# Retention and wave-MLP on one core: the first batch's pairs interleaved, idle products at the start, casts on other engines

## The chip, the cores and the metric

One core of a Trainium2 chip. The metric is the time of one execution on the device in microseconds (us): the median of several runs. The engines are called by the names of the profile: PE (TensorE, matrix products), DVE (VectorE), ACT (ScalarE), POOL (GpSimd) and SP (SyncE, which issues the transfers).

## What is computed

The inputs are q, k and v of 4 batches, 8 heads, 768 positions and 64 columns, and four weight matrices. A retention layer is followed by a mixing layer:

```
gamma = 1 - 2 ** (-5 - h)                       # one decay per head
for t in range(768):
    state = gamma * state + outer(k[t], v[t])   # 64 x 64 per batch and head
    y[t]  = (1 / 8) * q[t] @ state
x = y, heads side by side                       # 4 x 768 x 512
theta = x @ w_theta
zr, zi = x * cos(theta), x * sin(theta)
u = x + w_tok_r @ zr + w_tok_i @ zi             # mixing over the 768 positions
out = u + max(u @ w_ch, 0)
```

## The kernel before, in words

The positions are cut into chunks of 128, six for each batch, 24 in all; n counts them (L56, L61). Inside a chunk the recurrence is written as products: scores k·q under a causal mask, scores times v, and q times the state that the chunks before have left. The decays are put into q and v as factors (`qsc`, `vsc`, and `qscp`, `vscp` for pairs), computed at the start with Exp on ACT. Products take bf16 operands and add up in PSUM.

**An order by hand.** The kernel asks for manual scheduling (L66): each engine works through its instructions in the order in which the program text issues them, and a pool of tiles with a fixed number of buffers makes an instruction wait until the tile that held the buffer before has been read. PSUM is divided by tags: "tr" (two buffers, all transposes), "acc" (two: values `yT_ps`, `th_ps`, and some y and o products), "at", "st" and "y" (one each).

**Loads.** All loads of the head are issued at once on SP, in the order of the string at L120 (p for a pair, c for a chunk, w for two row blocks of the token matrices, th and ch for the two others). The loads of a w must wait until one of the four buffers `wtok` has been cast by `w_cast`, and those behind them in SP's queue wait too.

**The first batch, in pairs.** The six chunks of batch 0 are taken as three pairs g = 0, 1, 2. A pair's 256 positions lie as 128 partitions times two neighbours, so that a load has longer rows. `pair_in(g)` (L512) does all of a pair:

- `pair_prep` (L212): cast of k (one POOL instruction of 1024 columns), scaling of q and of v (two POOL instructions of 512 columns each).
- `pair_T` (L224): eight PE transposes of k or q to PSUM, one DVE copy back (`kqT`, L231).
- `pair_A(g, two)` (L234): sixteen small score products, then the mask multiply on DVE (L247). There is one PSUM buffer for scores, so the second set waits for the first mask.
- `pair_Y(g)` (L252): for both halves sixteen value products (L262); then for each chunk a of the pair in turn the four products with the state (L274), the eight products that add to the state (L282), two casts of the state by ACT into `stbd` (`state_out`, L296, L299), and the cast of the values to `xT` by ACT (L292).

Then `att_X(n)` (L367) follows for each chunk: four transposes of xT (L373) with a DVE copy to `x_sb` (L379), four products with w_theta (L376), and two sines on ACT, cos and sin (L381, L382). `att_Z` (L385) multiplies them with x on DVE into `z` (L387).

**Token matrices.** `w_cast(t0)` (L445) casts two row blocks on POOL into three buffers `wrow`; `w_tok(t0)` (L451) transposes them with twelve PE instructions (L455), and a DVE copy (wtr, L461) and an ACT copy (wti, L459) put them in place.

**Mixing.** `moe_M(m, lo, hi)` (L394) adds two y products per chunk of positions (L405), each 512 columns wide, and at the end u = y + x on DVE (L410). `moe_U` (L413) transposes u, `moe_O` (L426) multiplies with w_ch (L433), and DVE forms the output (L436), which SP stores.

**The order of the head**, L524 to L552: pair 0, the cast of w_theta on DVE (L525), `att_X` of chunks 0 and 1, pair 1, and so on, with y products of m = 0 and 1 put between as soon as their z and w are there. In the pairs 1 and 2 the z of the chunk before stands on DVE between the copies of k and q.

**The slot loop**, from L573: slot s does the scores of chunk n = 6 + s, the values of the chunk before, x and the sines of the one before that, z of the one before that, and one mixing row m in two halves. POOL scales chunk n + 1 (`att_prep`, L184 to L189). In slots 1, 3 and 5 `w_tok(3)`, `w_tok(4)` and `w_tok(5)` stand at L615, behind the products and ahead of the slot's `att_X`. `moe_U` stands at L595, ahead of `att_Yinter` (L323).

## Time and profile before

| | us |
|---|---|
| median of 9 runs (199.04 to 200.37) | 200.0 |
| the profiled execution | 199.31 |
| its span, first to last instruction | 197.5 |
| PE busy in the span | 164.2 |
| DVE / ACT / POOL busy | 105.1 / 76.3 / 77.1 |
| first score product of pair 0, 1, 2 | 10.44, 25.84, 42.50 |
| first y product of the slot loop | 61.41 |

A span is the profile's time base, and the profiled execution's own time is 1.81 us longer than it. The landmarks come from the timeline, which lists an engine's instructions in order of time: start, length, line, tile written <- tiles read, sizes, and in brackets how long the engine had been idle and which engine's instruction ended that. The stages list, for each stretch, busy time and number of instructions of PE, PEld (loads of the stationary operand), DVE, ACT and POOL, then the granted clock, the transfers' busy share and GB/s. The waits list who waited for whom: total, times, longest.

### The profile page before, as it was taken

The page shows a single profiled execution, that of the slowest core. Times are in us where ns is not written, and L with a number is a line of the kernel's source. Part 1 is how long each engine was busy: PE and PEld are TensorE (multiplying, and loading weights), DVE is VectorE, ACT ScalarE, POOL GpSimd, SP SyncE. Part 2 cuts the span into 40 slices and gives each one's busy share as a digit, 9 for nine tenths or more (in the row PEclk, how much of TensorE's full clock was granted, in tenths as well). Part 3 has the DMA queues.
Part 4 walks back from the last instruction along what each step waited for, and adds up shares of the span by engine and source line. Part 5 has one row for each costly group of instructions (what it writes and reads, how often), then busy time and mean ns, then how long its engine had stood idle before and what let it go on. Part 6 is the DMA issues. An engine that isn't in the chain of part 4 may idle for free.

```text
span 197.5 us, 3773 instructions
## 1 busy us (share of the span) xinstructions
PE 164.2 (83%) x1484; PEld 96.4 (49%) x1508; DVE 105.1 (53%) x147; ACT 76.3 (39%) x142; POOL 77.1 (39%) x107
## 2 busy tenths in 40 slices
PE   0447628945897897997999999999999999999991
PEld 0335425534553564654565566555555444444460
DVE  1162470362246747676787668666565554542451
ACT  4005804622531587536464464425643453200010
POOL 6849680300189882999255526525000000000000
PEclk9999985695799999999999999999999999999997
DMA  5999995199499999989496895994457446233343
GB/s 154 328 307 336 319 309 139 22 264 300 108 209 229 283 191 226 271 227 227 94 227 127 177 202 144 192 213 106 110 131 81 106 106 108 81 108 112 101 136 108
DMA packets 85906, 35.64 MB, mean 180 GB/s; under 512 B 70912, under 2 KB 80384, under 8 KB 85888
## 3 DMA queue, kind: packets, MB, share of 16 engines
q1 hardware_dynamic: 85744, 35.27, 77.5%
q8 instruction: 12, 0.20, 0.4%
q10 hardware_dynamic: 144, 0.13, 0.2%
q14 instruction: 6, 0.05, 0.1%
HBM read 25.69 MB, written 6.29 MB: 162 GB/s over the span
## 4 chain that ended last, share of the span: by engine, by line
PE 74%; DVE 9%; ACT 7%; DMA 3%; issue 3%; POOL 1%; DVEq 0%; SPq 0%; ACTq 0%; POOLq 0%
PE y_ps L405 29%; PE o_ps L433 10%; PE th_ps L376 10%; DVE at L247 4%; PE yT_ps L340 3%; DMA pair<-in_q_dram 3%; PE at_ps L311 3%; PE x_ps L373 2%; PE st_ps L282 2%; PE kq_ps L198 2%; PE w_ps L455 2%; ACT stbd L299 2%; PE st_ps L348 2%; DVE z L387 2%; PE at_ps L243 2%
## 5 line engine op out<-in xcount | busy, mean ns | idle before, releaser
L405 PE MATMUL y_ps<-z,wti 128*128 128x512 bf16 x136 | 52.0, 383 | 0.9 <-issue 0.4
L405 PE MATMUL y_ps<-z,wtr 128*128 128x512 bf16 x126 | 48.0, 381 | 1.1 <-DVE z L387 0.6
L381 ACT ACTIVATE cs<-th_ps,halfpi 128x512 bf16<-128x512 f32 x24 | 16.5, 688 | 36.1 <-PE th_ps L376 33.7
L387 DVE TENSOR_TENSOR z<-cs,x_sb 128x1024 bf16<-128x1024 bf16 x24 | 19.4, 807 | 16.2 <-ACT cs L382 16.2
L376 PE MATMUL th_ps<-wth,xT 128*128 128x512 bf16 x89 | 26.4, 407 | 0.7 <-issue 0.4
L299 ACT CAST stbd<-st_ps 64x256 bf16<-64x256 f32 x40 | 14.7, 366 | 30.0 <-PE st_ps L282 29.5
L315 DVE TENSOR_TENSOR at<-at_ps,mask 128x1024 bf16<-128x1024 f32 x18 | 21.9, 1219 | 5.6 <-PE at_ps L311 5.6
L433 PE MATMUL o_ps<-wch,uT 128*128 128x512 bf16 x89 | 23.2, 379 | 0.4 <-ACT cs L382 0.3
L410 DVE TENSOR_TENSOR u<-y_ps,x_sb 128x512 bf16<-128x512 f32 x23 | 15.8, 690 | 12.0 <-PE y_ps L405 11.8
L189 POOL TENSOR_TENSOR vb<-vf,vsc 128x512 bf16<-128x512 f32 x18 | 19.2, 1068 | 6.1 <-PE yT_ps L340 5.0
L448 POOL CAST wrow<-wtok 128x768 bf16<-128x768 f32 x12 | 9.8, 826 | 28.8 <-issue 27.2
L405 PEld LDWEIGHTS <-wti 128*128 128x128 bf16 x138 | 13.6, 98 | 15.3 <-issue 2.4
L436 DVE SCALAR_TENSOR_TENSOR ot<-o_ps,u 128x512 f32<-128x512 f32 x23 | 15.8, 690 | 9.8 <-PE o_ps L433 9.7
L405 PEld LDWEIGHTS <-wtr 128*128 128x128 bf16 x138 | 13.6, 98 | 13.6 <-issue 0.3
L187 POOL TENSOR_TENSOR kqb<-qf,qsc 128x512 bf16<-128x512 f32 x18 | 19.7, 1095 | 0.0
L186 POOL CAST kqb<-kf 128x512 bf16<-128x512 f32 x18 | 11.5, 637 | 18.9 <-issue 14.1
L379 DVE COPY x_sb<-x_ps 128x512 bf16<-128x512 bf16 x19 | 7.9, 418 | 18.0 <-PE x_ps L373 18.0
L382 ACT ACTIVATE cs<-th_ps,zerob 128x512 bf16<-128x512 f32 x24 | 16.4, 681 | 0.0
L356 ACT CAST xT<-yT_ps 128x512 bf16<-128x512 f32 x18 | 10.6, 587 | 11.8 <-PE yT_ps L340 11.6
L201 DVE COPY kqT<-kq_ps 128x1024 bf16<-128x1024 bf16 x13 | 9.0, 691 | 9.3 <-PE kq_ps L198 9.3
L433 PEld LDWEIGHTS <-uT 128*128 128x128 bf16 x92 | 8.8, 98 | 10.3 <-issue 0.6
L376 PEld LDWEIGHTS <-xT 128*128 128x128 bf16 x96 | 9.4, 107 | 8.0 <-issue 2.1
(73 smaller groups left out, 196.1 us busy)
## 6 DMA issues: line engine op xcount, KB each, us to landing
out_dram<-ot SPq DMA_DIRECT2D x23, 256.0 KB, 2.2
kf<-in_k_dram SPq DMA_DIRECT2D x18, 256.0 KB, 4.8
qf<-in_q_dram SPq DMA_DIRECT2D x18, 256.0 KB, 5.1
vf<-in_v_dram SPq DMA_DIRECT2D x18, 256.0 KB, 4.9
wtok<-in_moe_w_tok_r_dram SPq DMA_DIRECT2D x6, 384.0 KB, 5.5
wtok<-in_moe_w_tok_i_dram SPq DMA_DIRECT2D x6, 384.0 KB, 5.2
pair<-in_k_dram SPq DMA_DIRECT2D x3, 512.0 KB, 8.2
pair<-in_q_dram SPq DMA_DIRECT2D x3, 512.0 KB, 9.1
```

Of the source, the lines that this page charges most:

```text
L187: nc.gpsimd.tensor_mul(qb.rearrange(r3, h=H), raw[n, "qf"], _bcast_last(qsc[:, c], D))
L189: nc.gpsimd.tensor_mul(vb.rearrange(r3, h=H), raw[n, "vf"], _bcast_last(vsc[:, c], D))
L299: nc.scalar.copy(stbd[(c + 1) % 2][sl, :, sl], st_ps[b][sl, :, sl])
L315: nc.vector.tensor_mul(at.rearrange("p a j t -> p (a j) t"), at_ps.rearrange("p a j t -> p (a j) t"), _bcast_mid(mask, H))
L376: nc.tensor.matmul(th_ps, s["xT"][:, j, :], wth[:, j, :], start=(j == 0), stop=(j == NP - 1))
L381: nc.scalar.activation(cs[:, 0, :], th_ps, AF.Sin, bias=halfpi, scale=1.0)
L382: nc.scalar.activation(cs[:, 1, :], th_ps, AF.Sin, bias=zerob, scale=1.0)
L387: nc.vector.tensor_mul(zs[b][:, c], st[n]["cs"], _bcast_mid(xs[b][:, c, :], 2))
L405: nc.tensor.matmul(y_ps, wT[r][:, s0, t0 * P:(t0 + 1) * P], zs[b][:, s0, r, :], start=(s0 == 0 and r == 0), stop=(s0 == nT - 1 and r == 1))
L410: nc.vector.tensor_add(u, y_ps, xs[b][:, t0, :])
L433: nc.tensor.matmul(o_ps, mo[m]["uT"][:, j, :], wch[:, j, :], start=(j == 0), stop=(j == nD - 1))
L436: nc.vector.scalar_tensor_tensor(ot, o_ps, 0.0, mo[m]["u"], ALU.max, ALU.add)
```

## The change

- The slot loop's `w_tok` of slots 1, 3, 5 is issued ahead of `moe_O`, `att_Yinter` and the scores; `moe_U` is issued behind `att_Yinter`.
- k of a pair is cast by ACT instead of POOL. One half of q is scaled by DVE, the other by POOL. v stays on POOL. The values of a pair's second chunk are cast to xT by DVE, those of the first by ACT. w_theta is cast by POOL instead of DVE.
- A Sin of one column (`sin0`) is issued right behind the four Exp, so that ACT loads the table of the sines there.
- `pair_Y` is split into `pair_Y(g, two)`, `pair_I` (products with the state), `pair_S` (state products and casts) and `pair_out` (cast to xT), and the head's order is written out in these pieces. The state products now stand before the value products of the same pair, and a pair's second scores come after the first state products.
- `keep_busy(times)` issues products of a zeroed tile, 128 x 512, into the PSUM buffer that y takes later; nobody reads them. There are 30: 12 at the very start, the others between the pieces of pairs 0 and 1.

```diff
+    warm = const.tile([P, dm], BF)
+    nc.vector.memset(warm, 0.0)
...
+    sin0 = const.tile([P, 1], FT)
+    nc.scalar.activation(sin0, zerob, AF.Sin, bias=zerob, scale=1.0)
...
         if name == "k":
-            nc.gpsimd.tensor_copy(dst, src)
-        else:
-            for two in range(2):
-                sc = (qscp if name == "q" else vscp)[:, 2 * g + two]
-                nc.gpsimd.tensor_mul(dst[:, two], src[:, two], _bcast_last(sc, D))
+            nc.scalar.copy(dst, src)
+        for two in range(2):
+            if name == "q":
+                eng = (nc.vector, nc.gpsimd)[two]
+                eng.tensor_mul(dst[:, two], src[:, two],
+                               _bcast_last(qscp[:, 2 * g + two], D))
+            elif name == "v":
+                nc.gpsimd.tensor_mul(dst[:, two], src[:, two],
+                                     _bcast_last(vscp[:, 2 * g + two], D))
...
+    def pair_out(g, a):
...
+        (nc.vector.tensor_copy if a else nc.scalar.copy)(
+            xT.rearrange("e j (i w) -> e j w i", w=2),
+            yT.rearrange("e j (w i) -> e j w i", w=2))
...
+    def keep_busy(times):
+        for _ in range(times):
+            nc.tensor.matmul(warm_ps, warm[:, 0:P], warm, start=True, stop=True)
```

The head's new order (one call after the other; `kb` stands here for `keep_busy`, prep, T, A, S, Y, I, out for the `pair_` pieces, X, Z for `att_`, M for `moe_M`):

```
kb 12, prep 0k, T 0k, kb 4, prep 0q, T 0q, kb 2, prep 0v, cast w_theta,
A 0,0, kb 2, S 0,0, kb 1, A 0,1, S 0,1, Y 0,0, I 0,1, kb 3, prep 1k,
Y 0,1, out 0,0, out 0,1, kb 1, T 1k, prep 1q, X 0, X 1, T 1q, kb 2, prep 1v,
A 1,0, Z 0, w_cast 0, kb 2, S 1,0, A 1,1, Z 1, Y 1,0, I 1,0, prep 2k,
S 1,1, I 1,1, kb 1, Y 1,1, out 1,0, out 1,1, w_tok 0, T 2k, prep 2q,
X 2, X 3, M(0,0:2), T 2q, prep 2v, Z 2, A 2,0, M(0,2:3), w_cast 1,
A 2,1, S 2,0, Y 2,0, I 2,0, I 2,1, Y 2,1, out 2,0, out 2,1, Z 3, w_tok 1,
w_cast 2, att_prep 6, X 4, X 5, M(0,3:4), Z 4, M(1,0:4), w_tok 2,
M(0,4:5), M(1,4:5), att_T 6, Z 5, M(0,5:6), M(1,5:6)
```

And in the slot loop:

```diff
-        if U_at.get(s_, M_DMA) < M_DMA:
-            moe_U(U_at[s_])
+        if s_ in (1, 3, 5):
+            w_tok(3 + s_ // 2)
         if U_at.get(s_ - 1, 0) >= M_DMA:
             moe_O(U_at[s_ - 1])
         if s_ - 1 in n_of:
             att_Yinter(n_of[s_ - 1])
+        if U_at.get(s_, M_DMA) < M_DMA:
+            moe_U(U_at[s_])
...
-        if s_ in (1, 3, 5):
-            w_tok(3 + s_ // 2)
         if s_ - 2 in n_of:
             att_X(n_of[s_ - 2])
```

## The prediction

> **What bounds the kernel now.** I read the page's parts 1 and 2 first, to see where TensorE (PE) is idle, then the stages, then PE's waits in the head, then the timeline.

> ```profile
> PE 164.2 (83%) x1484; PEld 96.4 (49%) x1508; DVE 105.1 (53%) x147; ACT 76.3 (39%) x142; POOL 77.1 (39%) x107
> ...
> PE   0447628945897897997999999999999999999991
> ...
> PEclk9999985695799999999999999999999999999997
> DMA  5999995199499999989496895994457446233343
> ```

> A slice is 4.9 us. From slice 20 (100 us) on PE is nearly full, so nothing but less PE work shortens that half. All that can be won lies in the first 16 slices.

> ```profile
> 5.00:10.00 5.00, 2.25 (x16) 1.59 (x17) 1.00 (x2) 0.00 (x0) 4.09 (x5) 1.00 1.14 329
> ...
> 25.00:30.00 5.00, 1.73 (x66) 1.27 (x66) 3.24 (x4) 0.00 (x0) 3.86 (x4) 0.83 1.04 285
> 30.00:35.00 5.00, 4.01 (x29) 2.82 (x31) 0.42 (x1) 2.41 (x6) 0.00 (x0) 0.50 0.54 130
> 35.00:40.00 5.00, 4.86 (x28) 2.99 (x28) 1.58 (x3) 3.35 (x6) 1.60 (x2) 0.65 0.22 49
> ```

> In the stages (PE's busy time comes first, then PEld, DVE, ACT, POOL; clock, DMA share and GB/s last), PE is busy 35.7 us of the first 60. The busy time in it is partly slow: at 30 to 35 the granted clock is 0.50. The transfers have gone down to 49 GB/s by 35 to 40: they wait for the kernel, not the kernel for them. PE's waits of the first 62 us name who it stands for:

> ```profile
> PE at_ps L243 <- DVE kqT L231: 5.0, 3, 2.7
> PE at_ps L243 <- DVE at L247: 4.0, 3, 1.4
> PE yT_ps L262 <- DVE at L247: 3.2, 3, 1.1
> PE yT_ps L274 <- ACT stbd L299: 2.7, 3, 0.9
> ```

> These are hand-overs inside one pair (transposes, copy, scores, mask, second scores, second mask, values, state), with no other work of PE in between. So the head is a chain of latencies, run three times. The timeline gives the second cost, the rate:

> ```profile
> 6.22 1.03 PE L228 MATMUL kq_ps<-ident,kqb 128*128 128x128 bf16 x8 [6.22 <-POOL kqb L217]
> ...
> 22.08 1.06 PE L228 MATMUL kq_ps<-ident,kqb 128*128 128x128 bf16 x16
> 23.91 1.27 DVE L387 TENSOR_TENSOR z<-cs,x_sb 128x1024 bf16<-128x1024 bf16 x1
> ```

> Eight transposes take at 6.22 what sixteen take at 22.08. By that spacing PE runs at half rate until 21.5, again from 29.3 to 37.7 and from 46.5 to 52. (The clock column's 1.00 at 5 to 10 doesn't show the first of these; the spacing decides.)

> [...] full rate came after the dense stretch 17.5 to 21.5, half rate after 23.1 to 29.3, where PE did 1.3 us of work between long waits. [...] z at 23.91 took 1.27 us, beside POOL's scaling of q, where z alone takes 0.69. [...] Here the load at 20.11 took 1.28 and the first use began at 21.40[...].

> **The change, part by part.** I walk each engine's new order: an instruction starts when its engine is free and 0.05 us after its last operand. Durations are rows of the timeline. PE at full rate, start to start: 8 transposes of a pair 0.445; 16 small score or value products 0.25; 8 state products 0.43 (half of their half-rate 0.86); 4 x transposes 0.22; 4 th products 0.86; a y or idle product 0.215; the last result of a group comes 0.17 later. Others: mask 1.23, kqT copy 0.69, a state's two casts 0.74, xT 0.74, two sines 1.28, wtr 0.56, wti 0.81, z 0.69; on POOL half a q 1.04, v 2.06, two w rows 1.6. As a control, the same walk with the old order and half rate where the trace shows it puts the first y product of the slot loop at 60.96; the trace has it at 61.41.

> *The unknown prices.* k's cast on ScalarE (ACT): by wch's rows, 0.613 for 512 columns, two of them 1.23 at most[...], I take 1.04. Half a q on DVE isn't in the trace: 0.69 (the u row, same size, from PSUM) alone, 1.73 if it waits out a POOL instruction of 1.04; I take 1.29, as z at 23.91 lost 0.58. wth on POOL: twice the 1.04 of a 1024-column cast, 2.08; th's landing takes 8.0 from its issue at 3.30, so 11.3 to 13.4, and q of pair 1 only lands at 15.0: nothing waits. The table load now stands ahead of k's cast: 3.95 + 1.28 + 0.28 = 5.5 while k lands at 5.1, so 0.4 us is paid there; at 20.11 it no longer delays the first sines.

> *Pair 0*: k cast 5.50 to 6.54 (POOL ended at 6.16), transposes 6.59, copy 7.25, DVE's half of q 7.96 to 9.25, transposes 9.30, copy 9.97, scores 10.71 (was 10.44), masks to 12.41 and 14.16. Nothing won yet. Values 14.38; ACT still casts k of pair 1 until 15.28, so xT at 15.30; x and th products at 16.09 and 17.17 (were 18.47 and 20.58).
> *Pair 1*: its k transposes go at 15.33, its q ones at 18.25 behind those th products; scores 19.66 (was 25.84), 21.41; z of chunk 0 stands between the two masks on DVE (0.99), second mask to 23.62; values 23.67 (was 29.33); w_tok, then x of chunks 2 and 3 at 26.16 and 27.24 (were 33.88 and 37.48).
> *Pair 2*: k transposes 25.72, q 29.18 behind y products, scores 30.59 (was 42.50), masks to 32.80 and 34.55 with z 2 ahead of them, values 34.76 (was 45.98), x of chunks 4 and 5 at 37.31 and 38.39 (were 51.14 and 53.87).
> *Rest*: y products of m = 1 from 39.94 (once chunk 4's sines have freed the bank), w_tok(2) 41.66, chunk 6's transposes 43.19. On DVE the kqT copy now stands ahead of z 5 (44.56 to 45.25), so the last products go at 45.30, u 46.38 to 47.07, and the slot loop's first product at **47.12**.

> So 60.96 - 47.12 = 13.8 us are won. The eighteen idle products behind the first twelve cost 3.9 us at full rate, and most fall into waits; the first twelve (12 x 0.43 = 5.2 us from about 1) end before k's transposes. Without that cover each costs 0.2.

> *Queues moved past.* The loads keep their order on SP, but those that wait for a w cast come earlier: the second row of w 2 is cast at 35.6 in the walk (53.34), which lets the loads behind it go. POOL does chunk 7's scaling by 45.7, needed in slot 1 at 48.8. The new DVE multiply holds up the DVE queue behind it (kqT of q, x copies), which the walk includes.

> *The slot loop*: w_tok of slots 1, 3, 5 goes ahead of the chunk's products. PE waits there now 0.48 (kq_ps for wtr), 0.89 (x_ps for wti), 1.33 (x_ps for wtr). In slots 1 and 3 the u transposes must then wait for wtr, which stands behind a u add: 0.69 + 0.56 less the 0.67 of w_tok, 0.6 us each; slot 5 has no u transposes. So -0.1, +0.3 and +1.3; I take 1.2, ends 0 and 2.2. wti ahead of xT and the state casts delays these 0.81, which the products in between hide.

> Sum: 197.5 - 13.8 - 1.2 = 182.5 span; with the 1.81 that lay around it, 184.3 against the profiled 199.31. The median of the runs is 0.69 above that: **185.0**.

> **The rivals.**
> *More waits than walked, 188 to 190.5*: half rate until 15 us moves the loop's start to 49.6 (+2.4); hand-overs of 0.1 and DVE's q waiting a full POOL instruction give 49.6 also. For it: POOL is without a break in 15 to 20; against it: the control missed by only 0.45.
> *Transfers take over, 191.8*: chunk 9's loads are issued at 54.6 to 57.3 and land some 5.4 later (the median of such loads early in the trace is 5.0 to 5.4), about 61.5; scaled by 64.2, but its transposes (71.72) would be due at 71.7 - 14.3 = 57.4, so if the loads come no earlier, +6.8. For it: DMA shares over 1.2 at 60 to 70. Against: w 2's cast frees these loads some 18 us earlier, and the shares of 30 to 40 and 50 to 55 leave about 11 us of transfers to be pulled forward.
> *The array stays at half rate, slower, 204.9*: the gaps of the new order and its idle products fail to hold the full clock in the head. Everything of PE there costs twice, the idle products too: the walk gives 67.0, so 185.0 + 19.9. It decides the sign once 15.0 of these 19.9 us, three quarters of the head's columns, run slow. Against it: the walk has PE busy about 75% between 10 and 43, and at 75 to 80 a share of 3.80 in 5 did not lose the full rate.
> *The idle products do nothing*, because the real work warms the array as at 21.5: that is the half-rate end of the first rival.

> **How the numbers follow.** Forecast 0.68 (181 to 188: no contention -1.2, loop 2.2 -1.0, scatter; upwards the half of the first rival), more waits 0.15, transfers 0.07, half rate 0.05, and 0.05 for a time below 181, where my prices are too high. 181 to 190.5 leaves out 0.17. Within 0.3% of before, which is about what a measurement of this kernel can tell from no change, lies 0.01; faster 0.94, slower 0.05.

> **What would show it.** In the profile after: pair 0's scores still near 10.7; eight transposes of pair 0 taking about 0.6 and not 1.03; scores of pair 1 near 19.7, of pair 2 near 30.6; the loop's first y product near 47; no wait of PE for wti or wtr ahead of x_ps in slots 3 and 5, but one of u_ps; from there to the end 135, against 136.1. A transpose spacing of 0.107 past 15 us, or PE idle behind POOL's kf or qf with a DMA as releaser, would make it wrong.

## The result and the profile after

The changed kernel takes 182.0 us in the median of 10 runs, the kernel before 200.0 in 31: a ratio of 0.911 (95% interval 0.909 to 0.913), 17.8 us. The prediction was 185.0, 181.0 to 190.5. The profiled execution took 183.03 with a span of 181.3. Ratios leave out executions more than 1.5% above the fastest of their kernel, medians don't, so the two can differ by up to 1.5% in what follows; gains are taken from ratios.

The page of the changed kernel, parts 1 and 2:

```profile
PE 164.4 (91%) x1511; PEld 94.2 (52%) x1538; DVE 108.5 (60%) x153; ACT 77.3 (43%) x143; POOL 74.8 (41%) x102
...
PE   7789885976989699999999999999999999999991
...
PEclk9999999699999999999999999999999999999997
DMA  5999999999999999999999999954463453334543
```

PE's busy time is what it was (164.4 after 164.2), although 30 idle products came in: in the head it now does more in the same time (eight transposes of pair 0 in 0.62, where they took 1.03). The gap of the transfers at slices 6 and 7 (counted from 0) has gone; they run without a break up to slice 25. The stages, with the columns as before:

```profile
25.00:30.00 5.00, 4.16 (x48) 2.56 (x46) 3.57 (x6) 2.63 (x5) 4.43 (x5) 1.00 1.03 301
30.00:35.00 5.00, 3.60 (x66) 2.48 (x62) 3.27 (x3) 0.73 (x2) 0.37 (x1) 0.76 0.89 218
35.00:40.00 5.00, 4.06 (x45) 2.67 (x43) 2.62 (x6) 2.83 (x5) 3.68 (x4) 0.90 0.97 212
```

PE is busy 4.16 between 25 and 30, where it was 1.73. Between 30 and 40 the granted clock still dips (0.76 and 0.90), in one short stretch where the old order had a long one (0.50 and 0.65). PE's waits of the first 60 us, the longest in total first:

```profile
PE y_ps L425 <- DVE z L407: 2.3, 2, 1.5
PE at_ps L251 <- DVE kqT L239: 1.5, 3, 0.8
PE y_ps L545 <- DVE warm L124: 1.3, 1, 1.3
PE x_ps L393 <- ACT wti L479: 0.9, 1, 0.9
PE at_ps L251 <- DVE at L255: 0.8, 2, 0.5
```

The hand-overs inside a pair (at_ps for kqT and for the mask) took 5.0 and 4.0 and now take 1.5 and 0.8; those of the values for mask and state (3.2 and 2.7) have left the list. The longest is a new one: y for the z of chunks 2 and 5. From the timeline, PE's lines that answer the prediction's landmarks:

```profile
6.54 0.62 PE L236 MATMUL kq_ps<-ident,kqb 128*128 128x128 bf16 x8 [0.56 <-ACT kqb L221]
...
10.00 0.42 PE L251 MATMUL at_ps<-kqT 64*64 64x128 bf16 x16 [0.35 <-DVE kqT L239]
...
19.21 0.42 PE L251 MATMUL at_ps<-kqT 64*64 64x128 bf16 x16 [0.35 <-DVE kqT L239]
...
29.69 0.42 PE L251 MATMUL at_ps<-kqT 64*64 64x128 bf16 x16 [0.78 <-DVE kqT L239]
...
45.36 0.38 PE L425 MATMUL y_ps<-z,wtr 128*128 128x512 bf16 x1 [1.47 <-DVE z L407]
...
46.73 0.81 PE L425 MATMUL y_ps<-z,wtr 128*128 128x512 bf16 x2 [0.35 <-DVE u L430]
```

| | before | walked | after |
|---|---|---|---|
| scores of pair 0 | 10.44 | 10.71 | 10.00 |
| scores of pair 1 | 25.84 | 19.66 | 19.21 |
| scores of pair 2 | 42.50 | 30.59 | 29.69 |
| first y product of the slot loop | 61.41 | 47.12 | 46.73 |
| from there to the end of the span | 136.1 | about 135 | 134.6 |

So 14.7 us come from the head and 1.5 from the rest. Eight transposes of pair 0 take 0.62, as at 28.30 (0.61), and not the 1.03 of the kernel before: the array was at full rate by then.

### The profile page after: what moved, and what is told of

The parts are those of the page before. It is cut to its first block, busy times and chain, and to the rows that moved or that the text cites. A ratio compares the mean times of both kernels' runs of the same rounds, so it can differ in the third digit from the quotient of the medians.

```text
span 181.3 us, 3837 instructions
## 1 busy us (share of the span) xinstructions
PE 164.4 (91%) x1511; PEld 94.2 (52%) x1538; DVE 108.5 (60%) x153; ACT 77.3 (43%) x143; POOL 74.8 (41%) x102
## 4 chain that ended last, share of the span: by engine, by line
PE 80%; ACT 8%; DVE 7%; issue 3%; DVEq 0%; POOL 0%; POOLq 0%; ACTq 0%
PE y_ps L425 31%; PE o_ps L453 11%; PE th_ps L396 11%; PE yT_ps L360 3%; PE at_ps L331 3%; PE kq_ps L202 3%; PE st_ps L368 3%; PE x_ps L393 2%; PE yT_ps L349 2%; PE u_ps L436 2%; PE kq_ps L236 2%; PE y_ps L495 1%; PE st_ps L308 1%; PE w_ps L475 1%; DVE at L255 1%
## 5 line engine op out<-in xcount | busy, mean ns | idle before, releaser
L401 ACT ACTIVATE cs<-th_ps,halfpi 128x512 bf16<-128x512 f32 x24 | 16.5, 687 | 35.0 <-PE th_ps L396 32.7
L396 PE MATMUL th_ps<-wth,xT 128*128 128x512 bf16 x90 | 24.0, 379 | 0.3
L453 PE MATMUL o_ps<-wch,uT 128*128 128x512 bf16 x88 | 23.1, 379 | 0.2
L191 POOL TENSOR_TENSOR kqb<-qf,qsc 128x512 bf16<-128x512 f32 x18 | 19.2, 1069 | 5.2 <-DMA qf<-in_q_dram 5.1
L468 POOL CAST wrow<-wtok 128x768 bf16<-128x768 f32 x12 | 11.1, 937 | 10.2 <-PE w_ps L475 7.2
L396 PEld LDWEIGHTS <-xT 128*128 128x128 bf16 x96 | 8.6, 98 | 6.8
L438 ACT COPY uT<-u_ps 128x512 bf16<-128x512 bf16 x12 | 7.0, 586 | 9.1 <-PE u_ps L436 9.1
```

The source lines that it names most:

```text
L191: nc.gpsimd.tensor_mul(qb.rearrange(r3, h=H), raw[n, "qf"], _bcast_last(qsc[:, c], D))
L396: nc.tensor.matmul(th_ps, s["xT"][:, j, :], wth[:, j, :], start=(j == 0), stop=(j == NP - 1))
L401: nc.scalar.activation(cs[:, 0, :], th_ps, AF.Sin, bias=halfpi, scale=1.0)
L453: nc.tensor.matmul(o_ps, mo[m]["uT"][:, j, :], wch[:, j, :], start=(j == 0), stop=(j == nD - 1))
```

## The experiments

All times are medians in us; each ratio is against the kernel before, run on the same chip. The changed kernel's ratio is 0.911.

**Without the idle products** (the changed kernel, all 30 taken out).

```diff
-    keep_busy(12)
...
-    keep_busy(4)
...
```

> The changed kernel without any of its 30 idle products (nothing else differs). Theory: the real work alone lets the array to full rate only near 20 us, as in the old order; the walk then starts the slot loop at 50.0 instead of 47.0, so about 185 us (+3.0 over the changed kernel's 182.0), and the first scores' stage shows eight transposes in 1.03 us. Rival 1, the denser order warms the array by itself before 10 us: 182.0 to 183. Rival 2, the idle products carry most of the gain: the array falls back again in the pairs, 190 or more.

Measured: 183.5, ratio 0.9196 (0.9165 to 0.9226). The idle products are worth 1.7 us. PE in this kernel's timeline:

```profile
6.55 1.03 PE L236 MATMUL kq_ps<-ident,kqb 128*128 128x128 bf16 x8 [6.55 <-ACT kqb L221]
...
17.60 1.24 PE L396 MATMUL th_ps<-wth,xT 128*128 128x512 bf16 x4
18.68 0.39 PE L393 MATMUL x_ps<-ident,xT 128*128 128x128 bf16 x4
...
21.26 0.42 PE L251 MATMUL at_ps<-kqT 64*64 64x128 bf16 x16 [0.78 <-DVE kqT L239]
...
46.76 0.38 PE L425 MATMUL y_ps<-z,wtr 128*128 128x512 bf16 x1 [0.35 <-DVE u L430]
```

Eight transposes take 1.03 at 6.55, four take 0.63 at 17.18 and 0.39 at 18.68: full rate comes between 17.6 and 18.7, by the real work, near the 20 that the theory had. Scores of pair 1 start 2.05 later than with the idle products (21.26, 19.21), of pair 2 1.7 later. The slot loop, walked to 50.0, starts at 46.76: level with the profile above, which had a spell of half rate in pair 2, and 1.1 behind a second profile of the changed kernel without that spell (45.64, further down). About 0.7 of the delay was made up in pair 2, where DVE did z of chunk 2 in 0.68 (1.36 and 1.34 in the two profiles with the idle products). The theory's mechanism holds, its size (3.0) was too large: both rivals fall.

**Idle products alone, in the old order** (the kernel before with the zeroed tile, `keep_busy` and this edit to `pair_in`; 44 in all, none in pair 2).

```diff
+        kb = keep_busy if g < 2 else (lambda times: None)
+        if g == 0:
+            kb(12)
         pair_prep(g, "k")
         pair_T(g, "k")
+        kb(4)
...
         pair_T(g, "q")
+        kb(4)
         pair_prep(g, "v")
         pair_A(g, 0)
+        kb(4)
         pair_A(g, 1)
+        kb(4)
         pair_Y(g)
```

> The kernel before, in its old order, with idle products only: 12 at the start and four after each step of the pairs 0 and 1 (28 more); none in pair 2, where the PSUM buffer is in use. Theory: full rate up to about 46 us; the old order walked wholly at full rate starts the slot loop at 53.4 instead of 61.0, pair 2 stays partly slow, so 4 to 7.5 us of gain, 192.5 to 196. Rival, warmth is worth nothing without the interleaving because the waits for DVE and ACT set the time: 199 to 200. Rival 2, warmth is most of the change: 186 or less.

Measured: 196.0, ratio 0.9772 (0.9729 to 0.9815): 4.6 us, near the lower end of the theory. (The four products after each of eight steps are 32; the expectation counted 28.) In its timeline the full rate holds through pair 0 (eight transposes in 0.62 at 6.21, and in 0.61 still at 20.64). In pair 1 it is lost from 24.8 to 28.2, after PE has waited 2.1 for a kqT copy, although idle products stand after each step (four of them take 1.69 and 1.74 there, 1.03 before); in pair 2, where there are none, it goes again:

```profile
40.24 0.42 PE L245 MATMUL at_ps<-kqT 64*64 64x128 bf16 x16 [1.32 <-DVE at L249]
40.46 0.42 PE L264 MATMUL yT_ps<-at,kqb 64*64 64x128 bf16 x16
41.98 0.64 PE L264 MATMUL yT_ps<-at,kqb 64*64 64x128 bf16 x16 [1.10 <-DVE at L249]
```

Sixteen value products take 0.42 at 40.46 and 0.64 at 41.98. The hand-overs (1.32 and 1.10 for the mask) are as long as in the kernel before (1.32 at 44.24, 1.10 at 45.98): the idle products didn't take them away.

**The new order alone** (no idle products, old engines for the casts, no early Sin, old slot loop).

> Only the new order of the head: no idle products, the casts on their old engines, no early Sin, the slot loop's old order. Theory: the interleaving is the main part of the change; with half rate until 18 to 22 the walk starts the slot loop at 48.5 to 50.4, against 61.0 of the old order and 47.1 of the change: 185 to 186.5. Rival, the parts need one another and the order alone gives less than half of the 18 us: 191 or more.

Measured: 187.1, ratio 0.9225 (0.9166 to 0.9285), that is 184.5 by the ratio: 15.5 us of the 17.8. This ratio rests on two of the six runs; the median of all six gives 12.9. In the profile, one of the other four, the slot loop starts at

```profile
49.58 0.81 PE L423 MATMUL y_ps<-z,wtr 128*128 128x512 bf16 x2 [0.35 <-DVE u L428]
```

11.8 earlier than before, although the array fell to half rate in pair 1 (from 26.6) and in pair 2 (from 36.7). By each of these figures interleaving is the main part. By ratio it lies 0.5 below the theory's range, by the median 0.6 above it; the rival is out. The gains of the order and of the idle products in the old order (4.6) overlap, so they are not to be added: the new order reaches full rate by itself, between 19 and 20 in this profile. But it doesn't hold it there (mean granted clock 0.977; 1.000 in the two runs behind the ratio).

**Casts back on their old engines**, order and idle products as changed.

```diff
-            nc.scalar.copy(dst, src)
+            nc.gpsimd.tensor_copy(dst, src)
...
-                eng = (nc.vector, nc.gpsimd)[two]
+                eng = nc.gpsimd
...
-        (nc.vector.tensor_copy if a else nc.scalar.copy)(
+        nc.scalar.copy(
...
-    nc.gpsimd.tensor_copy(wth, wdma["th"])
+    nc.vector.tensor_copy(wth, wdma["th"])
```

> The changed kernel with the casts back on their old engines (k and both halves of q on POOL, w_theta on DVE, both xT on ACT); order and idle products as changed. Theory: the casts' spread is worth little, since the walk of it starts the slot loop at 47.5 instead of 47.1: 182.4. Rival, POOL becomes the bound of the pairs (k, q and v in a row take 5.2 us a pair) and the spread is a main part of the gain: 185 or more.

Measured: 184.3, ratio 0.9199 (0.9168 to 0.9231): the spread is worth 1.8, not 0.4, and not the 3 and more of the rival. PE's longest wait in this kernel is

```profile
PE at_ps L251 <- DVE at L255: 2.5, 3, 1.7
```

with 1.7 in pair 0: the second scores go at 13.67 (11.81 in the changed kernel). DVE's cast of w_theta stands ahead of the first mask in this order and begins at 11.26, released by w_theta's transfer; the mask follows at 12.40 (10.53 in the changed kernel). The walk of this variant had not held DVE up for it. In this profile 0.7 of the delay is left where the slot loop starts (46.37, against 45.64 in the second profile of the changed kernel), so how the 1.8 is shared between the casts stays open.

**The slot loop's old order**, with the head as changed.

> The changed kernel with the slot loop's old order (w_tok of slots 1, 3 and 5 behind the products, moe_U ahead of att_Yinter); the head as changed. Theory: the waits of the old loop come back (0.5, 0.9 and 1.3 us) and those of the new one go (0.6 and 1.5), so between -0.6 and +1.5 us against 182.0, with +0.6 the likeliest: 182.6. The prediction priced it at +1.2. Rival, the order is worth more than its waits: 184 or more.

Measured: 184.5, ratio 0.9141 (0.9108 to 0.9174): 0.6 slower by ratio, with overlapping intervals, so between nothing and 1.2. Its trace has the old waits back: x_ps for wtr 1.3, kq_ps for wtr 0.5, x_ps for wti 0.9 twice (one of them in the head). The rival's 184 isn't supported by the ratio.

**No early Sin** (`sin0` and its tile taken out).

> The changed kernel without the one early Sin, so that the sines' table is loaded at the first sine of chunk 0, as in the old order. Theory: the early load costs 0.4 us ahead of k's cast and saves nothing on the path, because the first sines have 1.4 us of slack before z of chunk 0 is due; without it 181.6, or no difference that can be told. Rival: the load of 1.28 us at the first sines delays the values' banks and z, 183 or more.

Measured: 183.2, ratio 0.9156 (0.9115 to 0.9197). Neither side is settled: the interval touches that of the changed kernel and reaches 183.9. A gain from taking it out is not to be seen.

**Where the gain of the slot loop went.** The prediction had a wait of 0.6 in slot 3. The changed kernel's waits of PE from 46 us to the end show

```profile
PE u_ps L436 <- ACT wti L479: 1.5, 1, 1.5
PE u_ps L436 <- DVE wtr L481: 0.6, 1, 0.6
```

the 0.6 for wtr in slot 1, and 1.5 for wti in slot 3. On ACT, wti stands behind the four casts of w_ch (0.61 each) of slot 2. To test this, they were issued in slot 0:

```diff
-        if s_ == 2:
+        if s_ == 0:
             wch_cast(0, nD)
```

> The changed kernel with one move: the four casts of w_ch on ACT are issued in slot 0, where ACT has nothing to do, instead of slot 2. Theory: PE's wait of 1.5 us for wti in slot 3 comes from these casts, which stand ahead of it on ACT; it shrinks to the 0.6 of slot 1, so about 181.1 (-0.9). Rival, the wait is only shifted, because wtr then comes last or w_ch has not landed by slot 0 and holds up ACT: 182 or slower.

Measured: 182.5, ratio 0.9081 (0.9033 to 0.9128), overlapping that of the changed kernel. The time can't tell; the trace can. From the same list for this kernel:

```profile
PE u_ps L436 <- DVE wtr L481: 1.1, 2, 0.6
```

No wait of u_ps for wti is left in the loop; slot 3 waits 0.5 for wtr, slot 1 0.6. The cause is shown, its worth in time (0.9) isn't.

**Two waits in the head.** The y products at 45.36 waited 1.47 for z of chunk 5, which stands behind chunk 6's kqT copy on DVE (seen in the walk too); and x of chunk 4 waited 0.9 for wti of `w_tok(1)`. The first edit alone, then the second alone, then both with the move of w_ch's casts, and the changed kernel once more beside them:

```diff
-    att_T(nT)
     att_Z(nT - 1)
+    att_T(nT)
```

```diff
+    w_cast(1)
     pair_A(2, 0)
+    w_tok(1)
     moe_M(0, 2, 3)
-    w_cast(1)
     pair_A(2, 1)
...
     att_Z(3)
-    w_tok(1)
     w_cast(2)
```

> The changed kernel unaltered, beside the other three on one chip: 182.0, with single runs from 181 to 186 as the half-rate spell in pair 2 (32.7 to 36 us in its profile) comes or not.

> The changed kernel with only z of chunk 5 issued ahead of chunk 6's transposes. Theory: PE's wait of 1.47 us for that z goes, the loop starts 1.5 earlier, 180.5; the spell of half rate in pair 2 and so the scatter of the runs stay. Rival: chunk 6's kqT copy or u comes last in its place, under 0.5 of gain.

> The changed kernel with only w_tok(1), its twelve transposes, put between the two score sets of pair 2. Theory: they fill PE's idle time there, so the 0.9 us wait for wti ahead of x of chunk 4 goes and 0.7 us of transposes leave the path, 1.5 in all, 180.5; and the array keeps full rate through pair 2, so that single runs scatter by about 1 us and not by 4. Rival: the spell comes from something else, the scatter stays.

> The move of w_ch's casts, and two more: z of chunk 5 is issued ahead of chunk 6's transposes (DVE does it before the kqT copy), and w_tok(1) goes between the two score sets of pair 2, with w_cast(1) ahead of them. Theory: the walk starts the slot loop at 44.2 instead of 47.1, and slot 3 gives 0.9 more: 182.0 - 3.9 = 178.1. Rival, the time is taken back: w's second cast and POOL's scaling of chunks 6 and 7 come last, or the transfers do, 180 to 182.

| | median | lowest to highest | ratio and interval |
|---|---|---|---|
| changed kernel again | 183.5 | 182.1 to 186.2 | 0.9136 (0.9091 to 0.9181) |
| z of chunk 5 first | 181.5 | 180.1 to 184.2 | 0.9049 (0.9015 to 0.9084) |
| w_tok(1) between the scores | 181.0 | 180.8 to 181.8 | 0.9052 (0.9027 to 0.9077) |
| three moves | 179.0 | 178.3 to 179.4 | 0.8946 (0.8916 to 0.8976) |

Each of the two is worth 1.7 us against the changed kernel run beside it (1.5 expected each), and 1.2 against the 0.911 of its first ten runs. With z first, the wait of 1.47 has gone and the loop starts at 45.42, 1.3 before the first profile of the changed kernel (both with the spell, mean granted clocks 0.989 and 0.985). With w_tok(1) between the scores it starts at 44.21, 1.43 before the second profile of the changed kernel, but not by the sum that was expected (0.9 of wait and 0.7 of transposes). The wait for wti has gone, and x of chunk 4 waits 0.82 for xT in its place. Another 0.6 comes from z of chunk 2 on DVE, here in the first profile of the changed kernel and then in the one with w_tok(1):

```profile
29.55 1.36 DVE L407 TENSOR_TENSOR z<-cs,x_sb 128x1024 bf16<-128x1024 bf16 x1
```

```profile
29.57 0.68 DVE L407 TENSOR_TENSOR z<-cs,x_sb 128x1024 bf16<-128x1024 bf16 x1
```

Both ran while POOL was casting rows of w. In the first POOL's three casts took 2.36, as long as undisturbed (two took 1.60 in the kernel before), and DVE was late; in the second DVE was not, and POOL's four casts took 3.68 where four of 0.82 make 3.3. In the profile with four moves, which has the same order here, z took 1.10. So this part is not a sure gain of the edit.

Together with w_ch's move the two give 179.0, 3.3 us better than the changed kernel and 21 better than the kernel before. The expectation was 178.1; of its rival nothing shows, the first y product of the loop goes at 42.81 (44.2 walked). PE in this kernel, where the twelve transposes fill the gap between the scores:

```profile
29.77 0.42 PE L251 MATMUL at_ps<-kqT 64*64 64x128 bf16 x16 [0.78 <-DVE kqT L239]
30.12 0.84 PE L475 MATMUL w_ps<-ident,wrow 128*128 128x128 bf16 x12
...
31.51 0.42 PE L251 MATMUL at_ps<-kqT 64*64 64x128 bf16 x16
...
33.71 0.42 PE L271 MATMUL yT_ps<-at,kqb 64*64 64x128 bf16 x16
```

The second scores now follow without a listed wait, and sixteen value products take 0.42. In the profile of the changed kernel they took 0.64 there:

```profile
32.10 0.42 PE L251 MATMUL at_ps<-kqT 64*64 64x128 bf16 x16 [0.54 <-DVE at L255]
32.45 0.94 PE L308 MATMUL st_ps<-kqb 64*128 64x128 bf16 x8
33.32 0.64 PE L271 MATMUL yT_ps<-at,kqb 64*64 64x128 bf16 x16
```

In the second profile of the changed kernel, though, they did not:

```profile
32.05 0.42 PE L251 MATMUL at_ps<-kqT 64*64 64x128 bf16 x16 [0.54 <-DVE at L255]
32.40 0.62 PE L308 MATMUL st_ps<-kqb 64*128 64x128 bf16 x8
32.94 0.42 PE L271 MATMUL yT_ps<-at,kqb 64*64 64x128 bf16 x16
```

Same order, same start within 0.05, half rate in one execution and full rate in the other (mean granted clock 0.76 and 1.00 from 30 to 35); the first scores of the slot loop are at 48.12 in the one and 47.03 in the other, so that such a spell costs 1.1. With w_tok(1) in the gap the four single runs lie within 1.0 of each other, the six of the changed kernel beside them within 4.1: what the theory of that run asked for. The mean granted clock was under 0.99 in 5 of 16 runs of the changed kernel and in none of the 15 of the three kernels with w_tok(1) there. Two things limit this. The gap is also shorter where z of chunk 2 takes 0.68; only the profile with four moves (z 1.10, no half rate in pair 2) speaks for the transposes alone. And the kernel without idle products, with nothing in this gap, stayed at 0.994 and above in all six runs, which is not explained.

**A fourth move**: `moe_U` behind the scores of the slot.

```diff
-        if U_at.get(s_, M_DMA) < M_DMA:
-            moe_U(U_at[s_])
         if n is not None:
             att_A(n)
+        if U_at.get(s_, M_DMA) < M_DMA:
+            moe_U(U_at[s_])
```

> The three moves (179.0) and a fourth: moe_U of the slot loop is issued behind the scores instead of ahead of them. Theory: in slots 1 and 3 PE does the eight score products (0.33) while wtr is still being copied, so the two waits of u_ps, 0.57 and 0.51, shrink to about 0.2 each: 178.3. Rival: uT comes later and moe_O waits for it, 179.0 or slower.

Measured: 179.0, ratio 0.8947 (0.8923 to 0.8972), no different from three moves. The waits of u_ps went from 1.1 to 0.7 in total, and PE's products with w_ch now wait 0.3 for uT, which they had not: the rival, a wait put in another place.

## Why the prediction was right, point by point

**The bound and the mechanism** were right: the head is a chain of hand-overs, and taking other work into it starts the slot loop 14.7 us earlier (13.8 forecast). The order alone gives most of the 17.8 us (15.5 by the ratio, 12.9 by the median).

**The walk** was late by 0.4 to 0.9 at each landmark. The mis-sized term is DVE's half of q, taken at 1.29 in pair 0. The changed kernel's DVE shows

```profile
7.81 0.73 DVE L225 TENSOR_TENSOR kqb<-pair,qscp 128x512 bf16<-128x512 f32 x1
...
25.92 1.24 DVE L225 TENSOR_TENSOR kqb<-pair,qscp 128x512 bf16<-128x512 f32 x1
```

0.73 in pair 0, where POOL was about to finish, and 1.24 only in pair 2, beside POOL's scaling of v. The prediction had named 0.69 alone, 1.73 behind a whole POOL instruction, and took 1.29. These prices were the author's estimates from rows of the trace of before (0.69, 1.04, z's loss of 0.58). In pair 0, where it counted, the lower end came, in pair 2 about the value taken, and 1.73 in none. The cost was only 0.05 where DVE and POOL overlapped by 0.2 (0.73 in pair 0, against 0.68 in pair 1, without overlap). k's cast on ACT took 1.03 (1.04 taken, an estimate), w_theta's on POOL 1.89 from 11.37 (2.08 from 11.3). The load of the sines' table took 1.28 from 3.97 and Sin's first use followed at 5.26, as priced.

**The half rate in pair 2** was not in the walk; it took back up to 1.1 of what the walk had too slow. Without it (second profile) the loop starts 1.1 earlier, at 45.64: there the walk, 1.5 late at the loop, was further off than the table shows, so that the close landmark of 46.73 is in part luck.

**From profile to median**: I added the 0.69 by which the median of before lay above its profile. After, the median lies 1.04 below the profile, which had caught that half-rate spell. These 1.7 are the larger part of the 3.0 by which the forecast was too high; the rest is 0.9 in the head and 0.3 in the loop.

**The slot loop**: 1.2 forecast, 1.5 in the spans. The forecast's own three terms (-0.1, +0.3, +1.3) add up to 1.5; no reason was given for taking 1.2. Slot 1 (0.6 for wtr) and slot 5 (the 1.33 gone) are as worked out. Slot 3 is wrong in its working: not wtr but wti came last, 1.5, because I followed the DVE queue and not ACT's, where w_ch's casts stand. PE's waits for wti and wtr in the loop fell from 2.7 to 2.1, by 0.6, and the run with the old slot order also says 0.6, not clear of nothing. So the near match of 1.2 and 1.5 is luck; what makes the other 0.9 of the span was not found.

**The idle products**: all thirty together gain 1.7. That the first twelve would bring the full rate was the author's estimate; its sign in the trace of before was the dense stretch 17.5 to 21.5. It came true: the eight transposes behind the twelve take 0.62. What the eighteen later ones cost or gain apart from the first twelve was not tried.

**The rivals**: transfers did not take over. POOL waits for the chunks' loads (5.1 us in all for q, 3.9 for k, 2.3 for v), but PE's list names no POOL instruction, so this stays hidden. The array did not stay at half rate (eight transposes of pair 0 in 0.62, mean granted clock of the span 0.985). Of the "more waits" rival, priced at 2.4 and more, little came: a spell of half rate, but in pair 2, where it had not been named, and 1.1.

## What to carry to other kernels

When a head is a chain of hand-overs, walk every engine's queue in the new order and check the walk on the old one; that gave the start of the main loop to 0.4 us out of 47 in one profile and to 1.5 in another. Follow each queue that an instruction is moved past to its end: the one wait forecast wrongly stood behind casts on an engine that the change hardly touched. Real work put into a gap fills it and comes off the path, and here the mean granted clock was 0.994 or more in all 15 runs that had it; idle products in the same gap were not tried.

## What the runs showed of the hardware

Half rate came back without a long pause. In the kernel before, products ran at half rate again at 29.3 (sixteen value products in 0.64, 0.42 at 27.80), with no wait of PE over 2.70 since full rate had come at 21.5. In the first profile of the changed kernel it began at about 32.6 (eight state products in 0.94 at 32.45, 0.62 at 21.85), when no wait of PE since 28.3 had been longer than 0.86; up to there PE had about 1.4 us of products in 4.2 (transposes 0.44, scores 0.25 twice, y 0.43). What came ahead of it was a low share of work, 1.4 in 4.2, and not a long wait. That is not a sure sign either, because in the second profile the same stretch kept the full rate (eight state products in 0.62 at 32.40). With the twelve transposes added (0.67 more, 2.0 in the 3.5 to 3.9 up to the same point) half rate did not appear there in any of three profiles (mean granted clocks 0.994, 0.999 and 1.000 over the span).

Where DVE's half of q or its z ran beside POOL's work, one of the two took longer, or both. In pair 2 of the changed kernel DVE's half of q took 1.24 (0.68 in pair 1, without overlap) and POOL's two instructions for v beside it 2.49 (2.05 and 2.04 in pairs 0 and 1). z took 1.36 beside POOL's casts in one profile and 0.68 in another, where POOL's four casts took 3.68 instead of 3.3, with starts of z 0.02 us apart.
